# Two attention + gMLP layers on one core: VectorE's share of the exponentials as two addends instead of five, planner latencies split, and another spread of units

## The chip, the cores and the metric

The kernel runs on one core of one Trainium2 chip. Five engines run from queues of their own and wait for each other on semaphores: TensorE (PE), VectorE (DVE), ScalarE (ACT), GpSimd (POOL) and SyncE (SP, which issues the DMAs). The metric is the device time of one execution in microseconds, lower is better; times given are medians of several executions.

## The reference, cut to what matters

An attention and a gMLP are applied in turn, twice (two layers, the same weights), to x of 2048 tokens and 512 channels. The attention has 32 query heads of 16 channels that share one key head and one value head:

```python
q = (x @ wq).reshape(B, S, 32, 16).transpose(0, 2, 1, 3)
k = x @ wk                       # one key head for all query heads
v = x @ wv
scores = einsum('bhqd,bkd->bhqk', q, k) * 16 ** -0.5
p = softmax(scores, axis=-1)
o = einsum('bhqk,bkd->bhqd', p, v)
A(x) = o.transpose(0, 2, 1, 3).reshape(B, S, 512) @ wo
# B: z = gelu(x @ w_in); z1, z2 = halves; z2 = layernorm(z2)
#    g = w_sp @ z2 + b_sp;  B(x) = (z1 * g) @ w_out
x = x + A(layernorm(x)); x = x + B(layernorm(x))     # twice
```

For each layer the softmax needs 32 x 2048 x 2048 exponentials, 134 million. They are the largest piece of elementwise work by far.

## The kernel before, in words

**Groups, units, blocks.** The queries of one layer are cut into 32 groups; a group is 2048 columns of (head, query), held as four row groups of 512 columns. The 2048 keys are 16 tiles of 128. A *unit* is one group against one key tile: four score matmuls, each of which gives one *block* of 128 keys x 512 columns in one PSUM bank. Two layers have 2 x 32 x 16 = 1024 units and 4096 blocks. The first four groups of a layer (`attn_first`) run while keys and values are still being made, in stretches of key tiles that `KEYS` lists; the other 28 (`attn_rest`) run one after another over all 16 key tiles.

**Who takes the exponential.** Most units go through `push_unit`: ACT reads two or three banks at once (two slots, of three and of two banks) and writes exp of them as bf16 into `P_ring` (line 824), and PE then multiplies the block by the values `V_aug` into the accumulator bank `PVB` (line 841). The tables `ON_DVE`, `UNITS` and `FIRST_DVE` name the units that go through `push_unit_dve` instead, 160 of them, 80 in each layer: one in each of the first four groups, three in each of the next twenty, two in each of the last eight.

**How DVE makes an exponential.** For each of the four blocks one `tensor_scalar` (line 872) adds a constant to the scores in PSUM and writes the result as int16 into a tile of `big`. Scores are already scaled so that 128 units are one power of two; the int16 pattern read as bf16 is then 2 to the power of the score, with the fraction taken linearly. To mend that, four more tiles are made from the first by adding 26, 51, 77 and 102 to the int16 patterns (line 881, 128x2048 each), and PE sums all five tiles with values that carry the weights `PH_W` (`V_ph`, line 887): five passes of four matmuls for each unit. The ring of tiles in `big` has six tiles (five in the last eight groups).

**What sets the order.** Nothing is ordered by hand. `_Graph.schedule` simulates the engines with a duration `dur` and a latency `lat` for each operation, takes at each moment the ready operation with the lowest priority number, and so writes one fixed instruction list for each engine; semaphores keep it right whatever the true durations. When PE would idle too long it puts in fillers (`add_zeros`, line 639, which add zero to the accumulator, and the matmuls of ones at line 631). `dve` gives VectorE's operations a duration and no latency; the exponential has `0.065 + n * 0.4267`; a PSUM bank comes free when the latencies of all its operations are over.

**Beside the attention** DVE also normalises (lines 709 to 725), evacuates the output of a group (line 935; line 932 in the first groups), and serves the gMLP: projections (1051, 1077), statistics (1124, 1126, 1131), spatial mixing (1176), and the late mixing (1216, 1221, partly on POOL) after the last group. ACT takes the gelus in place (1087, 1107, 1115).

Of the kernel before, what the change touches and what calls it, by code (L numbers as in the profile page):

```python
# [10 lines left out]
ALU = mybir.AluOpType  # L11
# [25 lines left out]
TILED = 0.217  # L37
SWITCH = 0.105
PE_LAT = 0.20
SEM_LAT = 0.06  # L40
BESIDE = 0.03

HOLDS = 2.5

# [31 lines left out]
class _Op:  # L76
    __slots__ = ("eng", "fn", "dur", "lat", "prio", "seq", "deps", "succ", "nleft", "chan", "chan_val",
                 "inc", "pos", "val", "clock", "t0", "task", "mode", "rows", "work", "opens", "nstart", "due", "chain")

    def __init__(self, eng, fn, dur, lat, prio, seq, chan, task, mode):  # L80
        self.task = task
        self.mode = mode
        self.rows = frozenset()
        self.work = dur
        self.opens = None
        self.eng = eng
        self.fn = fn
        self.dur = dur
        self.lat = lat
        self.prio = prio  # L90
# [12 lines left out]
        self.nstart = 0  # L103
        self.due = 0.0


class _Graph:
# [66 lines left out]
    def schedule(self):  # L174
# [154 lines left out]
        while True:  # L329
            moved = True  # L330
            while moved:
                moved = False
                for e in ENGS:
                    if free[e]:
# [25 lines left out]
                        push(now + us + o.lat + SEM_LAT, 1, o)  # L360
                        at = now + us + o.lat + SEM_LAT
# [11 lines left out]
            while ev and ev[0][0] <= now + 1e-9:  # L373
                _, _, what, x = heapq.heappop(ev)
                if what == 0:
                    free[x] = True
                elif what == 1:
                    for s, k in x.succ:
                        if k == 1:
                            met(s, x)  # L380
                    t = x.task
                    if t is not None:
                        t.left -= 1
                        if t.left == 0:
                            for b in t.banks:
                                bank_free[b] = True
# [75 lines left out]
def bass_interleave_layers__grouped_kv_mqa__mixer_gmlp__prompt_kernel(  # L462
# [127 lines left out]
    def dve(fn, us, r, w, prio=5):  # L590
        return op("dve", fn, us, r=r, w=w, prio=prio)
# [211 lines left out]
    def push_slot(n):  # L803
# [22 lines left out]
        main["last"] = op("act", act_e, 0.065 + n * 0.4267, r=[tk], w=[("P", s0 + k) for k in range(n)], prio=3)  # L826
# [32 lines left out]
    def push_unit_dve(u):  # L859
# [3 lines left out]
        tiles = [phr["base"] + (phr["n"] + a) % phr["ring"] for a in range(NPH)]  # L863
        phr["n"] += NPH
        first_op = None
        for j in range(4):
# [7 lines left out]
                0.66, [tk], BIG(tiles[0]) if j == 0 else [("phj", tiles[0], j)], P_R)  # L874
# [5 lines left out]
        for a in range(1, NPH):  # L880
            dve(lambda e, a=a: e.tensor_scalar(ph16[:, tiles[a], :], ph16[:, tiles[0], :], float(PH_A[a]), None,  # L881
                                               op0=ALU.add), 0.63, base, BIG(tiles[a]), 4)
        for a in range(NPH):
            def pe_pv(e, a=a):
                ins = None
                for j in range(4):
                    ins = e.matmul(bank32(PVB)[32 * j:32 * j + 32, :], V_ph[:, a, kt, :],  # L887
                                   big[:, tiles[a], j * QC:(j + 1) * QC], tile_position=(0, 32 * j), start=False,
                                   stop=False)
                return ins  # L890
            pv_op(pe_pv, (base if a == 0 else BIG(tiles[a])) + [("V", kt)], False, False, TILED)
# [390 lines left out]
    UNITS = {0: (), 1: (4,), 2: (3, 8), 3: (2, 6, 10), 4: (2, 5, 8, 11)}  # L1282
# [6 lines left out]
    FIRST_DVE = ({12: (2,)}, {12: (2,)})  # L1289
# [13 lines left out]
    ON_DVE = [0] * NFIRST + [3] * 20 + [2] * 8  # L1303
# [64 lines left out]
```

## Time and profile before

| | |
|---|---|
| time, median of 3 (range) | 1753.39 us (1752.82 to 1754.59) |
| span of the profiled execution, first to last instruction | 1750.5 us |
| median less that span | 2.9 us |
| PE / DVE / ACT / POOL busy | 95% / 77% / 94% / 5% |
| granted TensorE clock, mean | 0.997 |
| exponentials on ACT, instructions and busy | 1383, 1571.3 us |
| exponentials on DVE, instructions and busy | 1280, 838 us |
| blocks on ACT / on DVE | 3456 / 640 |

The profile shows one execution. Its span is 1750.5 us; the time of an execution holds some microseconds around the span, and the median is 2.9 us above it. A busy share is a mean over stages: there are two stretches without exponentials, at the change of layers and at the end. Instructions of ACT and DVE overlap their successors a little, so a mean duration is longer than the distance between two starts. "PE busy" counts fillers and modelled ends.

### The profile page before, as it was taken

What the parts mean: (1) busy time and instruction counts of PE and PEld (TensorE: products, weight loads), DVE (VectorE), ACT (ScalarE), POOL (GpSimd) and SP (SyncE); (2) the same over time, 40 slices, a digit from 0 to 9 for tenths busy, and PEclk for the clock granted to TensorE, in tenths of its full rate; (3) what the DMA queues carried; (4) which work ended last, traced back from release to release, by engine and by line L of the source; (5) the groups of instructions that cost most, each with busy time, mean ns of one, the idle gap of its engine ahead of it and who ended that gap; (6) DMA issues with size and microseconds to landing.
All of it is one profiled execution on the core that took longest, in us unless ns stands there. A gap on an engine that the chain in (4) does not pass through costs nothing.

```text
span 1750.5 us, 44624 instructions
## 1 busy us (share of the span) xinstructions
PE 1664.3 (95%) x20010; PEld 579.3 (33%) x20010; DVE 1356.0 (77%) x2457; ACT 1637.6 (94%) x1425; POOL 90.4 (5%) x142
## 2 busy tenths in 40 slices
PE   8899999999999999999999999999999999999989
PEld 4332233332333333333432222333333333333334
DVE  8668788888877778675775987888888887766767
ACT  7999999999999999999659999999999999999970
POOL 2000000000000000000430000000000000000012
PEclk9999999999999999999999999999999999999999
DMA  6841000000100302335410000000000112033263
GB/s 185 225 103 49 1 1 2 1 2 25 41 14 20 106 23 70 124 96 161 144 53 19 2 2 1 2 1 2 7 26 7 53 46 88 15 110 110 98 224 120
DMA packets 94816, 104.22 MB, mean 60 GB/s; under 512 B 39072, under 2 KB 64288, under 8 KB 94624
## 3 DMA queue, kind: packets, MB, share of 16 engines
q1 hardware_dynamic: 94624, 101.37, 18.5%
q8 instruction: 156, 2.56, 0.6%
q14 instruction: 36, 0.29, 0.1%
HBM read 61.51 MB, written 39.85 MB: 58 GB/s over the span
## 4 chain that ended last, share of the span: by engine, by line
ACT 75%; PE 22%; DVE 1%; DMA 1%; issue 0%; SPq 0%; POOL 0%; DVEq 0%
ACT P_ring L824 73%; PE ps_all L613 6%; PE ps_all L800 6%; PE ps_all L618 4%; PE ps_all L841 3%; PE ps_all L887 2%; ACT z2n L1087 1%; PE ps_all L639 1%; ACT z1c L1115 0%; PE ps_all L721 0%; DVE big L1216 0%; DVE xn L714 0%; DMA X<-in_A_x_dram 0%; DVE big L1176 0%; DMA big<-gp_scratch 0%
## 5 line engine op out<-in xcount | busy, mean ns | idle before, releaser
L824 ACT ACTIVATE P_ring<-ps_all 128x1536 bf16<-128x1536 f32 (+1 forms) x1383 | 1571.3, 1325 | 56.5 <-PE ps_all L800 55.2
L800 PE MATMUL ps_all<-qT,kT_rep 32*128 32x512 bf16 x4096 | 637.5, 385 | 69.1 <-ACT P_ring L824 55.8
L872 DVE TENSOR_SCALAR big<-ps_all 128x512 int16<-128x512 f32 x640 | 421.8, 686 | 84.5 <-PE ps_all L800 80.2
L881 DVE TENSOR_SCALAR big<-big 128x2048 int16<-128x2048 int16 x640 | 416.2, 682 | 25.0 <-PE ps_all L887 23.8
L800 PEld LDWEIGHTS ps_all<-qT,kT_rep 32*128 32x128 bf16 x4096 | 159.1, 91 | 586.4 <-ACT P_ring L824 451.7
L841 PE MATMUL ps_all<-P_ring,V_aug 128*32 128x512 bf16 x3456 | 333.4, 389 | 0.8 <-DVE big L926 0.5
L887 PE MATMUL ps_all<-big,V_ph 128*32 128x512 bf16 x3200 | 265.0, 385 | 0.6 <-DVE big L872 0.4
L841 PEld LDWEIGHTS ps_all<-P_ring,V_aug 128*32 128x32 bf16 x3456 | 84.6, 93 | 180.7 <-issue 167.2
L639 PE MATMUL ps_all<-ones,zeros 128*32 128x512 bf16 x1320 | 115.0, 388 | 0.0
L887 PEld LDWEIGHTS ps_all<-big,V_ph 128*32 128x32 bf16 x3200 | 75.8, 95 | 90.5 <-issue 36.1
L613 PE MATMUL ps_all<-xnTA,z2n 128*32 128x512 bf16 x1344 | 92.5, 381 | 0.0
L697 POOL TENSOR_SCALAR ve<-mv 128x1 f32<-128x1 f32 (+3 forms) x40 | 10.6, 266 | 1577.3 <-DVE mv L710 1349.9
L962 DVE TENSOR_TENSOR X<-ps_all,X 128x512 bf16<-128x512 f32 x64 | 44.1, 688 | 40.0 <-PE ps_all L618 26.8
L935 DVE CAST oT<-ps_all 128x512 bf16<-128x512 f32 x56 | 38.7, 690 | 38.2 <-PE ps_all L841 38.0
L1176 DVE TENSOR_TENSOR big<-ps_all,big 128x512 f32<-128x512 f32 x56 | 38.3, 689 | 36.8 <-PE ps_all L613 36.5
L1176 DVE TENSOR_TENSOR big<-ps_all,bsp 128x512 f32<-128x512 f32 x56 | 38.5, 688 | 25.1 <-PE ps_all L613 24.6
L613 PE MATMUL ps_all<-w_in_r,xo 128*32 128x448 bf16 x960 | 57.3, 354 | 0.1
L618 PE MATMUL ps_all<-w_out_r,z1c 128*128 128x512 bf16 x224 | 54.2, 380 | 2.8 <-DVE z1c L1221 2.8
L1051 DVE CAST z2n<-ps_all 128x448 bf16<-128x448 f32 x60 | 37.4, 624 | 24.4 <-PE ps_all L613 22.6
L613 PE MATMUL ps_all<-xo,w_in_r 128*32 128x256 bf16 (+1 forms) x1120 | 52.4, 316 | 0.0
L618 PE MATMUL ps_all<-big,z2n 128*128 128x512 bf16 (+1 forms) x224 | 49.4, 366 | 1.3 <-DVE z2n L1131 1.3
L1077 DVE CAST z1c<-ps_all 128x512 bf16<-128x512 f32 (+2 forms) x56 | 36.6, 657 | 16.4 <-PE ps_all L613 13.6
(97 smaller groups left out, 1130.8 us busy)
## 6 DMA issues: line engine op xcount, KB each, us to landing
gp_scratch<-big SPq DMA_DIRECT2D x112, 256.0 KB, 2.0
big<-gp_scratch SPq DMA_DIRECT2D x105, 256.0 KB, 3.0
z1c<-in_B_w_sp_dram SPq DMA_DIRECT2D x16, 512.0 KB, 5.6
wspt_scratch<-z1c SPq DMA_DIRECT2D x16, 512.0 KB, 5.4
xnTA<-wspt_scratch SPq DMA_DIRECT2D x16, 384.0 KB, 4.1
big<-wspt_scratch SPq DMA_DIRECT2D x8, 512.0 KB, 5.8
z2n<-wspt_scratch SPq DMA_DIRECT2D x4, 768.0 KB, 4.8
z1c<-wspt_scratch SPq DMA_DIRECT2D x4, 768.0 KB, 5.6
```

The source lines that it names most:

```text
L613: ins = e.matmul(out_[32 * j:32 * j + 32, :], lhs[:, 32 * j:32 * j + 32], rhs, tile_position=(0, 32 * j), start=start, stop=stop)
L618: return e.matmul(out_, lhs, rhs, start=start, stop=stop)
L639: ins = e.matmul(bank32(PVB)[32 * j:32 * j + 32, :], zeros[:, 0:32], mv, tile_position=(0, 32 * j), start=False, stop=False)
L800: return e.matmul(out, kT_rep[32 * j:32 * j + 32, a, u[1] * P:(u[1] + 1) * P], qT[32 * j:32 * j + 32, q, :], tile_position=(32 * j, 0), st ...
L824: return e.activation(P_ring[:, s0:s0 + n, :], bank32(b0, n).rearrange("p (k q) -> p k q", k=n), ACTF.Exp, scale=E_SCALE)
L841: ins = e.matmul(bank32(PVB)[32 * j:32 * j + 32, :], V_aug[:, kt, :], P_ring[:, s, :], tile_position=(0, 32 * j), start=first, stop=last)
L872: o = dve(lambda e, j=j, tk=tk: e.tensor_scalar(ph16[:, tiles[0], j * QC:(j + 1) * QC], bank32(tk.bank), PH_BIAS, 0.0, op0=ALU.add, op1=AL ...
L881: dve(lambda e, a=a: e.tensor_scalar(ph16[:, tiles[a], :], ph16[:, tiles[0], :], float(PH_A[a]), None, op0=ALU.add), 0.63, base, BIG(tiles ...
L887: ins = e.matmul(bank32(PVB)[32 * j:32 * j + 32, :], V_ph[:, a, kt, :], big[:, tiles[a], j * QC:(j + 1) * QC], tile_position=(0, 32 * j), ...
L935: dve(lambda e: e.tensor_copy(oT[:, par, :], bank32(PVB)), 0.69, ["pvb"], [("oT", par)], 0)
L962: dve(lambda e: e.tensor_tensor(X[:, t, :], bank32(tk.bank), X[:, t, :], ALU.add), 0.69, [tk, ("X", t)], [("X", t)], prio)
L1176: dve(lambda e, part=part, tk=tk: e.tensor_tensor(part, bank32(tk.bank), part if st else bsp[:], ALU.add), 0.69, [tk] + ([] if st else ["b ...
```

## The change

The exponential on DVE gets another form. The bits are made as before, but with the bias 127 x 128 and without a correction. Two addends replace the five shifted tiles: the *whole power* (bits AND 0x7F80, that is 2^e), and the *bits times their own mantissa*: the mantissa as a number from 1 to 2 (bits AND 0x7F, OR 0x3F80), multiplied in bf16 with the bits read as bf16, which is 2^e (1+f)^2. PE sums the two with weights 0.671875 and 0.330078125, so a unit takes two passes of values instead of five, and two bitwise `tensor_scalar` and one `tensor_tensor` on 128x2048 instead of four additions. A unit holds three tiles of the ring instead of five.

181 units instead of 160 go to DVE, by a table for each layer and group. In layer 0 groups 4 to 23 have 71 units (60 before), groups 24 to 31 have 13 (16), and the first four groups two each (one). In layer 1 they have 65 (60), 20 (16), and one each as before.

The planner's figures change too: DVE's operations count 0.085 less as duration and get that as latency, the exponential becomes `0.051 + n * 0.4267` with a latency of 0.185, and a bank that ACT reads comes free without that latency.

```diff
-NPH = 5
-PH_A = (0, 26, 51, 77, 102)
-PH_W = (0.828125, 0.71875, 0.625, 0.54296875, 0.47460938)
+NPH = 2
+PH_W = (0.671875, 0.330078125)
-PH_BIAS = 127.0 * 128.0 - 128.0 * 2.102375911
+PH_BIAS = 127.0 * 128.0
+DVE_LAT = 0.085
+ACT_LAT = 0.185
+UNITS = {0: (), 1: (4,), 2: (3, 8), 3: (2, 6, 10), 4: (2, 5, 8, 11), 5: (2, 4, 7, 9, 12)}
+FIRST_DVE = ({4: (2,), 12: (2,)}, {12: (2,)})
+ON_DVE = ((0, 0, 0, 0, 3, 4, 3, 3, 4, 5, 3, 4, 4, 4, 4, 3, 4, 3, 4, 3, 3, 3, 3, 4, 2, 1, 3, 2, 1, 2, 1, 1),
+          (0, 0, 0, 0, 4, 4, 4, 4, 4, 3, 3, 2, 3, 3, 4, 4, 2, 3, 3, 2, 4, 2, 3, 4, 3, 2, 3, 1, 3, 3, 2, 3))
...
+                        if o.task is not None:
+                            push(now + us + (o.lat if o.free_lat is None else o.free_lat) + SEM_LAT, 3, o.task)
...
     def dve(fn, us, r, w, prio=5):
-        return op("dve", fn, us, r=r, w=w, prio=prio)
+        return op("dve", fn, max(us - DVE_LAT, 0.06), r=r, w=w, prio=prio, lat=DVE_LAT)
...
-        main["last"] = op("act", act_e, 0.065 + n * 0.4267, r=[tk], w=[("P", s0 + k) for k in range(n)], prio=3)
+        main["last"] = op("act", act_e, 0.051 + n * 0.4267, r=[tk], w=[("P", s0 + k) for k in range(n)], prio=3,
+                          lat=ACT_LAT)
+        main["last"].free_lat = 0.0
...
-        for a in range(1, NPH):
-            dve(lambda e, a=a: e.tensor_scalar(ph16[:, tiles[a], :], ph16[:, tiles[0], :], float(PH_A[a]), None,
-                                               op0=ALU.add), 0.63, base, BIG(tiles[a]), 4)
-        for a in range(NPH):
+        bits = ph16[:, tiles[0], :]
+        dve(lambda e: e.tensor_scalar(ph16[:, tiles[1], :], bits, 0x7F80, None, op0=ALU.bitwise_and), 0.69, base,
+            BIG(tiles[1]), 4)
+        dve(lambda e: e.tensor_scalar(ph16[:, tiles[2], :], bits, 0x7F, 0x3F80, op0=ALU.bitwise_and,
+                                      op1=ALU.bitwise_or), 0.69, base, BIG(tiles[2]), 4)
+        dve(lambda e: e.tensor_tensor(big[:, tiles[2], :], big[:, tiles[0], :], big[:, tiles[2], :], ALU.mult), 1.22,
+            base + BIG(tiles[2]), BIG(tiles[2]), 4)
+        for a in range(2):
             def pe_pv(e, a=a):
...
-                                   big[:, tiles[a], j * QC:(j + 1) * QC], tile_position=(0, 32 * j), start=False,
+                                   big[:, tiles[1 + a], j * QC:(j + 1) * QC], tile_position=(0, 32 * j), start=False,
...
-            on_dve = UNITS[ON_DVE[gi]]
-            phr["ring"] = NRING if gi < SHORT_RING else NPH
+            on_dve = UNITS[ON_DVE[now["layer"]][gi]]
+            phr["ring"] = NRING if gi < SHORT_RING else 5
...
-    UNITS = {0: (), 1: (4,), 2: (3, 8), 3: (2, 6, 10), 4: (2, 5, 8, 11)}
-    FIRST_DVE = ({12: (2,)}, {12: (2,)})
-    ON_DVE = [0] * NFIRST + [3] * 20 + [2] * 8
```

More of the change, by code (lines that the diff above doesn't have):

```diff
@@ L89, in __init__ @@
         self.lat = lat
+        self.free_lat = None
         self.prio = prio
@@ L380, in schedule @@
                             met(s, x)
[L381 to L386, printed above, removed]
+                elif what == 3:
+                    x.left -= 1
+                    if x.left == 0:
+                        for b in x.banks:
+                            bank_free[b] = True
         assert done == len(self.ops), (done, len(self.ops))
@@ L862, in push_unit_dve @@
         assert not first and not last
-        tiles = [phr["base"] + (phr["n"] + a) % phr["ring"] for a in range(NPH)]
-        phr["n"] += NPH
+        tiles = [phr["base"] + (phr["n"] + a) % phr["ring"] for a in range(3)]
+        phr["n"] += 3
         first_op = None
```

6 lines of the change are left out of this document (3 added, 3 removed).

## The prediction, written before the changed kernel ran

> **What bounds the kernel now.** I read the page's busy shares and chain first, then the costliest groups, the waits, and last the stretches of time by themselves.
>
> ```profile
> span 1750.5 us, 44624 instructions
> ...
> PE 1664.3 (95%) x20010; PEld 579.3 (33%) x20010; DVE 1356.0 (77%) x2457; ACT 1637.6 (94%) x1425; POOL 90.4 (5%) x142
> ...
> ACT 75%; PE 22%; DVE 1%; DMA 1%; issue 0%; SPq 0%; POOL 0%; DVEq 0%
> ...
> L824 ACT ACTIVATE P_ring<-ps_all 128x1536 bf16<-128x1536 f32 (+1 forms) x1383 | 1571.3, 1325 | 56.5 <-PE ps_all L800 55.2
> ...
> L872 DVE TENSOR_SCALAR big<-ps_all 128x512 int16<-128x512 f32 x640 | 421.8, 686 | 84.5 <-PE ps_all L800 80.2
> L881 DVE TENSOR_SCALAR big<-big 128x2048 int16<-128x2048 int16 x640 | 416.2, 682 | 25.0 <-PE ps_all L887 23.8
> ...
> L887 PE MATMUL ps_all<-big,V_ph 128*32 128x512 bf16 x3200 | 265.0, 385 | 0.6 <-DVE big L872 0.4
> ...
> L639 PE MATMUL ps_all<-ones,zeros 128*32 128x512 bf16 x1320 | 115.0, 388 | 0.0
> ```
>
> PE has the largest busy share, but the chain that ended last is 75% ACT, and ACT's exponentials sit idle for only 56.5 us in all. PE's 95% holds 115.0 us of fillers, which the planner writes only where PE would rest. The waits say which of the two waits for the other:
>
> ```profile
> PEld ps_all L800 <- ACT P_ring L824: 451.7, 1110, 2.0
> ...
> ACT P_ring L824 <- PE ps_all L800: 55.2, 31, 16.7
> ```
>
> The score matmuls wait 1110 times for ACT to free a slot; ACT waits 31 times for scores. Stretch by stretch, busy us and instructions (first PE, weight loads, DVE, ACT, POOL, the granted clock and the DMAs; then ACT's exponentials alone; then DVE's lines 872 and 881 alone):
>
> ```profile
> 125.00:605.00 480.00, 457.74 (x5647) 147.45 (x5646) 398.39 (x715) 478.26 (x420) 6.43 (x10) 1.00 0.06 20
> 220.00:393.00 173.00, 164.21 (x2073) 53.92 (x2069) 146.25 (x270) 172.89 (x151) 5.30 (x8) 1.00 0.01 2
> 985.00:1464.00 479.00, 458.51 (x5703) 149.19 (x5695) 397.25 (x712) 476.23 (x417) 5.72 (x10) 1.00 0.05 16
> ```
> ```profile
> 393.00:605.00 212.00, 211.94 (x189) 1.00 0.10 34
> ```
> ```profile
> 125.00:605.00 480.00, 160.13 (x243) 1.00 0.06 20
> 220.00:393.00 173.00, 52.36 (x80) 1.00 0.01 2
> 985.00:1464.00 479.00, 156.09 (x237) 1.00 0.05 16
> ```
> ```profile
> 125.00:605.00 480.00, 159.00 (x244) 1.00 0.06 20
> 220.00:393.00 173.00, 53.23 (x82) 1.00 0.01 2
> 985.00:1464.00 479.00, 159.03 (x244) 1.00 0.05 16
> ```
>
> 125 to 605 us is groups 4 to 23 of layer 0, 985 to 1464 the same of layer 1. ACT is busy for 99.6% of the one and 99.4% of the other. So a block taken from ACT is time saved, as long as DVE, at 83% in both, carries what it gets.
>
> **The price of a block on ACT.** From 393 to 605 us ACT does nothing but exponentials: 189 instructions, slots of three and two banks in turn, so 472.5 blocks in 211.94 us, 0.449 us each. The kernel's mean, 1571.3 us over 3456 blocks, is 0.455, with the small waits in it. I take 0.449. The change moves 181 - 160 = 21 units, 84 blocks: 37.7 us (38.2 by the mean). By place: four units more in layer 0's first groups (7.2 us), 11 more in its groups 4 to 23 (19.8), 3 fewer in 24 to 31 (minus 5.4); in layer 1, 5 more (9.0) and 4 more (7.2).
>
> **The price of a unit on DVE.** Back to back, operations start closer than they last:
>
> ```profile
> 1064.23 3.09 DVE L881 TENSOR_SCALAR big<-big 128x2048 int16<-128x2048 int16 x5
> ```
>
> (3.09 - 0.68) / 4 = 0.603 us for line 881; a block (line 872) lasts 4 ns longer, and I use 0.61 for both. A unit before is eight such, 4.9 us. After, the four block operations stay. The two bitwise ones have the shapes and types of line 881, and one of them has two operations in one instruction. The nearest rows for that, and for the product of two 16-bit tensors, are
>
> ```profile
> L1216 DVE TENSOR_TENSOR big<-ps_all,big 128x512 f32<-128x512 f32 x49 | 32.0, 681 | 5.0 <-PE ps_all L618 4.2 <-DMA big<-gp_scratch 0.8
> ...
> L1131 DVE TENSOR_SCALAR z2n<-z2n,mv,rs 128x896 bf16<-128x896 bf16 x32 | 14.7, 502 | 2.7 <-POOL rs L699 2.4
> ...
> L1216 DVE TENSOR_TENSOR big<-ps_all,big 128x256 f32<-128x256 f32 x7 | 2.6, 417 | 0.0
> ...
> L684 DVE TENSOR_TENSOR fold<-ident 128x64 bf16<-128x64 bf16 x1 | 0.2, 203 | 0.0
> ...
> L685 DVE TENSOR_TENSOR fold<-fold 128x32 bf16<-128x32 bf16 x1 | 0.2, 174 | 0.1
> ```
>
> Line 1216 costs (681 - 417) / 256 = 1.03 ns per element and 153 ns fixed; at that rate 2048 elements are 2.27 us. Line 881 streams 2048 in 682 - 153 = 529 ns, four times as fast. Line 1131 does two operations on 896 16-bit elements in 502 ns, where the slow rate would give 1.08 us, so two operations in one instruction don't lose the fast rate. Bitwise: between 0.68 and 2.27 us; I take 0.68, that of the row with the same operands. Product: between 0.68 (as one source) and 2.27 (line 1216's rate); I take 153 + 2 x 529 = 1.21, because two 16-bit sources must be read where line 881 reads one; less 0.07 of overlap, 1.14. A unit after: 6 x 0.61 + 1.14 = 4.8 us.
>
> Against my 1.21 speak lines 684 and 685, the only rows of such a product: 203 - 174 = 29 ns for 32 elements, 0.9 ns each, which would make 2.0 us and a unit 5.6. They are single records of short operations. The Trainium skill ("VectorE: DVE Perf Modes", section "The perf-mode tier table") holds that `tensor_tensor` on bf16 in SBUF goes at half of `tensor_scalar`'s top rate and gives 1224 ns for 2048 elements; no run here shows that yet. By the page the sum below stays as it is; by the two short rows it would be some 20 us higher, as worked out with the rivals.
>
> **DVE's load.** In 125 to 605 us DVE's other work is 398.39 - 160.13 - 159.00 = 79.3 us. With 71 units it needs 79.3 + 71 x 4.8 = 420 us; ACT needs 480 - 19.8 = 460. DVE is then 91% loaded, 96% if it keeps today's looser mean of (160.13 + 159.00) / 480 operations = 0.665 us. In layer 1: 397.25 - 156.09 - 159.03 = 82.1, plus 65 x 4.8, is 394 of 470 us, 84%. The tightest stretch is 220 to 393 us, groups 8 to 14: other work 40.7, units from 21 to 27, so 170 us of DVE work where ACT needs 173 - 6 x 1.8 = 162. That is 8 us too much. What can slide out of it is the normalising and projecting (lines 1051 to 1131) of tiles that are not mixed until later; the next groups have slack. I charge half, 4 us, as new waits of ACT; the ends are 0 and 20 (8 here, and some 12 in like stretches of four-unit groups that I can't tell apart from the trace).
>
> **PE.** Passes of values fall from 3200 to 1448 matmuls: 1752 at 265.0 / 3200 = 0.083 us, 145 us less; `P_ring`'s fall by 84. The instruction order has 1832 of line 639's fillers instead of 1320, 45 us. PE waits for ACT already, so I cost this at nothing: between minus 15 us (a bit less than half of the 55.2 - 16.7 = 38.5 us of ACT's waits for scores without the longest) and zero. What grows if DVE is late is PE standing at a pass of values, with the next scores behind it in PE's queue and ACT waiting for those; that is inside the 4 us above.
>
> **The last stage** changes only by its order:
>
> ```profile
> 1697.82 2.32 PE L631 MATMUL ps_all<-ones 128*128 128x512 bf16 x10
> 1699.97 0.59 PE L618 MATMUL ps_all<-w_out_r,z1c 128*128 128x512 bf16 x2
> 1703.37 5.79 PE L618 MATMUL ps_all<-w_out_r,z1c 128*128 128x512 bf16 x26 [2.80 <-DVE z1c L1221]
> ```
>
> Here PE burns 10 fillers and waits 2.80 us. In the new order eight real matmuls of the next part stand in place of most of those fillers: 8 x 0.22 = 1.8 us gained; between 0 and 4. The planner's split latencies change no instruction, only which comes first; elsewhere I cost that at nothing, between minus 5 and plus 5 us, because PE's and DVE's order is hidden as long as ACT has a full slot. No DMA is added or taken out on SP or POOL. A smaller `V_ph` (two weights) and fewer memsets are under 1 us, beside the first loads.
>
> **Sum.** 1750.5 - 37.7 + 4 - 1.8 = 1715.0 span; plus the 2.9 us that lie around it, 1718 us against the median of 1753.39, 2% faster.
>
> **The rivals.**
> *DVE can't keep up in the crowded groups.* All 20 us of DVE's excess become waits of ACT: 1718 + 16 = 1734. For it: 105% load from 220 to 393 us, and the passes of values are behind the evacuation of a group. Against it: the ring now holds two units, and neighbours with two or three units give the time back.
> *PE's relief shortens ACT's small waits.* Up to 15 us, so 1703. For it: ACT's mean of 0.455 against 0.449. Against it: fillers fill most of the room.
> *Slower: the new value operations don't run at the fast rate,* in groups 4 to 23 of layer 0. If the two bitwise take 153 + 2 x 529 ns, a unit is 4.8 + 1.06 = 5.9 us, DVE needs 79.3 + 71 x 5.9 = 498 us for the stretch instead of 460: 38 us more, and layer 1's 82.1 + 65 x 5.9 = 466 just fits its 470. That gives 1752, no change: at 5.9 us a unit the gain is gone. The product at line 1216's rate alone (1.06 more) makes the same; by lines 684 and 685 (0.8 more) it is 1718 + 22 = 1740. From there on it is slower: bitwise and product both so make 7.0 us, 116 us in layer 0 and 67 in layer 1, about 1900; the bitwise at the slow rate (1.59 more each) 8.0, 187 and 132 us, about 2035. For it: no row shows a bitwise operation. Against it: same operands as line 881.
> *The change doesn't do what it says:* the blocks leave ACT for certain, by count; what could fail is only their worth, which is the second and fourth case.
>
> **How the numbers follow.** Forecast (1708 to 1727) 0.61; DVE late (1727 to 1748) 0.16; small waits shorter (1697 to 1708) 0.10; slow rates, 0.13, of which 0.02 end within 0.2% (3.5 us, about what a measurement tells from no change) and 0.11 above. Faster 0.87, same 0.02, slower 0.11. The range from 1702 to 1748 leaves out the slow rates and the lowest part of the third case.
>
> **What would show it.** ACT: 1349 exponentials, about 1534 us busy, and idle before them still near 55 us (60 with the 4). Bitwise at 0.68 us and product near 1.21; 1.2 and 2.3 would mean the slow case. From 220 us on, more `ACT P_ring <- PE` waits if DVE is late, with PE standing at passes of values. DVE busy near 1440 us. The stage after the last exponential some 2 us shorter. I am wrong if the operations are slow, or if ACT's waits grow by more than 20 us.

## The result, and the profile after

The changed kernel takes 1727.58 us (median of 4, 1726.11 to 1728.45) against 1753.99 for the kernel before (the three executions of the table above and a fourth): a ratio of 0.9843, with a 95% interval from 0.9824 to 0.9863. The forecast was 1718 in a range from 1702 to 1748. So the direction and the range held, and 9.6 us are to be found. The profiled execution took 1728.45 us, its span 1726.7, which is 23.8 less than before. (One execution of one experiment, the planner's choice of closed fillers below, took 7195 us with each matmul some four times as long as in the others; it is left out of that experiment's time.)

The page of the changed kernel: busy time, the granted clock in 40 slices, the chain by engine, and the groups that answer to those shown before the prediction.

```profile
span 1726.7 us, 41922 instructions
...
PE 1623.9 (94%) x18678; PEld 558.7 (32%) x18678; DVE 1425.2 (83%) x2444; ACT 1602.1 (93%) x1391; POOL 93.7 (5%) x136
...
PEclk8899999999999999999998998999999999999999
...
ACT 74%; PE 20%; DVE 4%; issue 1%; POOL 0%; DMA 0%; SPq 0%; DVEq 0%
...
L832 ACT ACTIVATE P_ring<-ps_all 128x1024 bf16<-128x1024 f32 (+1 forms) x1349 | 1535.5, 1340 | 71.9 <-PE ps_all L808 70.5
...
L882 DVE TENSOR_SCALAR big<-ps_all 128x512 int16<-128x512 f32 x724 | 473.4, 683 | 50.1 <-PE ps_all L808 46.9
...
L895 DVE TENSOR_TENSOR big<-big 128x2048 bf16<-128x2048 bf16 x181 | 219.0, 1210 | 0.7
L647 PE MATMUL ps_all<-ones,zeros 128*32 128x512 bf16 x1832 | 161.7, 397 | 0.0
...
L901 PE MATMUL ps_all<-big,V_ph 128*32 128x512 bf16 x1448 | 131.0, 396 | 1.7 <-DVE big L895 1.0
L891 DVE TENSOR_SCALAR big<-big 128x2048 int16<-128x2048 int16 x181 | 123.3, 681 | 9.2 <-PE ps_all L901 8.2
L893 DVE TENSOR_SCALAR big<-big 128x2048 int16<-128x2048 int16 x181 | 122.6, 677 | 0.3
```

Line 832 is the old line 824, ACT's exponentials: 35.8 us less busy, and 15.4 us more idle before them (71.9 against 56.5), nearly all behind scores. Lines 891, 893 and 895 are the three new operations, 901 the passes of values (3200 matmuls before), 647 the fillers (1320 before). The stretches between the same evacuations (groups 4 to 23 of layer 0, groups 8 to 14 of it, groups 4 to 23 of layer 1) have these busy times, with the granted clock third from the end:

```profile
127.00:588.00 461.00, 429.27 (x4983) 139.96 (x4982) 435.92 (x731) 457.72 (x401) 9.46 (x10) 0.99 0.08 21
221.00:377.00 156.00, 143.04 (x1632) 44.67 (x1629) 150.11 (x245) 154.60 (x138) 3.16 (x2) 0.99 0.04 12
976.00:1450.00 474.00, 446.53 (x5306) 142.73 (x5303) 411.82 (x690) 468.26 (x410) 8.40 (x10) 0.98 0.06 19
```

In the tight stretch ACT is still busy for 154.60 of 156 us, so DVE, though itself busy for 96%, does not hold it up. What is new stands in the first 128 us. Two windows of the kernel before, then the same two after:

```profile
0.00:64.00 64.00, 55.13 (x646) 25.88 (x650) 51.72 (x116) 51.66 (x46) 11.75 (x36) 1.00 0.74 207
64.00:128.00 64.00, 58.28 (x655) 21.88 (x647) 40.05 (x70) 62.92 (x57) 0.00 (x0) 0.97 0.58 145
```
```profile
0.00:64.00 64.00, 56.01 (x551) 21.68 (x551) 53.37 (x114) 45.01 (x39) 8.84 (x28) 0.81 0.35 102
64.00:128.00 64.00, 58.84 (x641) 22.30 (x640) 54.00 (x90) 62.12 (x56) 1.26 (x2) 0.95 0.66 176
```

In the first window the granted clock falls from 1.00 to 0.81, ACT does 6.7 us less work, and PE is as busy as before. In the second DVE has 14 us more work than before; whether that matters is taken up with e12 below. In windows of 4 us:

```profile
32.00:36.00 4.00, 3.55 (x42) 1.37 (x40) 3.83 (x11) 4.00 (x4) 1.28 (x2) 1.00 0.62 135
36.00:40.00 4.00, 3.78 (x50) 2.20 (x46) 3.57 (x8) 4.00 (x5) 0.00 (x0) 1.00 0.76 213
```
```profile
28.00:32.00 4.00, 3.36 (x36) 1.18 (x36) 4.00 (x9) 4.00 (x4) 0.00 (x0) 0.99 0.14 31
32.00:36.00 4.00, 3.53 (x24) 0.78 (x24) 3.29 (x8) 3.76 (x5) 0.00 (x0) 0.50 0.02 4
36.00:40.00 4.00, 4.00 (x24) 0.61 (x23) 2.76 (x6) 2.81 (x3) 0.00 (x0) 0.50 0.00 0
40.00:44.00 4.00, 4.00 (x32) 2.16 (x29) 3.07 (x5) 2.61 (x3) 0.00 (x0) 0.50 0.00 0
```

The first pair is before, the rest after. From 32 us on the matmuls run at half rate: PE does 24 of them where it did 42 and 50, is "busy" for 3.53 and 4.00 of 4 us, and ACT, with 2.81 and 2.61 of 4 us, waits for scores. The clock's records give 11 such spells before the last exponential, 78.5 us in all; the kernel before has 10.2 us. Which comes first can be read from the trace: in the 3.4 us ahead of each of the 11 spells ACT is still busy for 99 to 100%, while PE is busy for only 44 to 82%, and ahead of ten of them what PE waits for longest is ACT, which has to free a slot (ahead of the one at 936 us it is DVE). So ACT does not lack scores before the clock falls; it lacks them after.

**Where the 23.8 us come from.** ACT's exponentials start 1.3305 us apart (three banks) or 0.9045 us (two) when nothing holds them; what is beyond that, from start to start, I count as wait. A wait is put down to a half-rate spell if the exponential ahead of it starts in the spell or in the microsecond behind it.

| | before | after | difference |
|---|---|---|---|
| exponentials at their own pitch | 1544.9 | 1507.3 | -37.6 |
| ACT's waits in half-rate spells | 4.4 | 27.5 | +23.1 |
| ACT's waits elsewhere | 35.4 | 31.2 | -4.2 |
| the one long wait at the change of layers | 16.8 | 16.3 | -0.5 |
| after the last group | 72.0 | 68.0 | -4.0 |
| all else (start, gelus) | 77.0 | 76.4 | -0.6 |
| span | 1750.5 | 1726.7 | -23.8 |

So the blocks gave what they were priced at, and against that stand 23 us more of waits that begin where PE's clock falls. The last stage, PE's rows of the changed kernel:

```profile
1717.01 0.82 PE L639 MATMUL ps_all<-ones 128*128 128x512 bf16 x3 [1.44 <-DVE big L1230]
1717.67 4.70 PE L626 MATMUL ps_all<-w_out_r,z1c 128*128 128x512 bf16 x21
```

Three fillers and a wait of 1.44 us stand where ten and 2.80 us stood.

### The profile page after: what moved, and what is told of

The parts are those of the page before. It is cut to its first block, busy times and chain, and to the rows that moved or that the text cites. A ratio compares the mean times of both kernels' runs of the same rounds, so it can differ in the third digit from the quotient of the medians.

```text
span 1726.7 us, 41922 instructions
## 1 busy us (share of the span) xinstructions
PE 1623.9 (94%) x18678; PEld 558.7 (32%) x18678; DVE 1425.2 (83%) x2444; ACT 1602.1 (93%) x1391; POOL 93.7 (5%) x136
## 4 chain that ended last, share of the span: by engine, by line
ACT 74%; PE 20%; DVE 4%; issue 1%; POOL 0%; DMA 0%; SPq 0%; DVEq 0%
ACT P_ring L832 73%; PE ps_all L621 6%; PE ps_all L808 5%; PE ps_all L626 4%; PE ps_all L851 3%; PE ps_all L901 1%; ACT z2n L1101 1%; PE ps_all L647 1%; DVE big L1230 1%; DVE st L1138 0%; DVE big L882 0%; DVE xn L722 0%; DVE z2n L1145 0%; DVE st L717 0%; PE ps_all L746 0%
## 5 line engine op out<-in xcount | busy, mean ns | idle before, releaser
L832 ACT ACTIVATE P_ring<-ps_all 128x1024 bf16<-128x1024 f32 (+1 forms) x1349 | 1535.5, 1340 | 71.9 <-PE ps_all L808 70.5
L808 PE MATMUL ps_all<-qT,kT_rep 32*128 32x512 bf16 x4096 | 653.3, 391 | 79.5 <-ACT P_ring L832 61.9
L882 DVE TENSOR_SCALAR big<-ps_all 128x512 int16<-128x512 f32 x724 | 473.4, 683 | 50.1 <-PE ps_all L808 46.9
L851 PE MATMUL ps_all<-P_ring,V_aug 128*32 128x512 bf16 x3372 | 325.6, 395 | 1.4 <-DVE oT L949 0.8
L895 DVE TENSOR_TENSOR big<-big 128x2048 bf16<-128x2048 bf16 x181 | 219.0, 1210 | 0.7
L647 PE MATMUL ps_all<-ones,zeros 128*32 128x512 bf16 x1832 | 161.7, 397 | 0.0
L901 PE MATMUL ps_all<-big,V_ph 128*32 128x512 bf16 x1448 | 131.0, 396 | 1.7 <-DVE big L895 1.0
L891 DVE TENSOR_SCALAR big<-big 128x2048 int16<-128x2048 int16 x181 | 123.3, 681 | 9.2 <-PE ps_all L901 8.2
L893 DVE TENSOR_SCALAR big<-big 128x2048 int16<-128x2048 int16 x181 | 122.6, 677 | 0.3
L647 PEld LDWEIGHTS ps_all<-ones,zeros 128*32 128x32 bf16 x1832 | 41.2, 95 | 74.0 <-issue 67.7
L621 PE MATMUL ps_all<-w_in_r,xo 128*32 128x448 bf16 x960 | 56.5, 355 | 0.5 <-DVE z1c L1091 0.3
L901 PEld LDWEIGHTS ps_all<-big,V_ph 128*32 128x32 bf16 x1448 | 36.1, 96 | 47.7 <-issue 24.1
```

The lines of the kernel that those rows point to most:

```text
L621: ins = e.matmul(out_[32 * j:32 * j + 32, :], lhs[:, 32 * j:32 * j + 32], rhs, tile_position=(0, 32 * j), start=start, stop=stop)
L647: ins = e.matmul(bank32(PVB)[32 * j:32 * j + 32, :], zeros[:, 0:32], mv, tile_position=(0, 32 * j), start=False, stop=False)
L808: return e.matmul(out, kT_rep[32 * j:32 * j + 32, a, u[1] * P:(u[1] + 1) * P], qT[32 * j:32 * j + 32, q, :], tile_position=(32 * j, 0), st ...
L832: return e.activation(P_ring[:, s0:s0 + n, :], bank32(b0, n).rearrange("p (k q) -> p k q", k=n), ACTF.Exp, scale=E_SCALE)
L851: ins = e.matmul(bank32(PVB)[32 * j:32 * j + 32, :], V_aug[:, kt, :], P_ring[:, s, :], tile_position=(0, 32 * j), start=first, stop=last)
L882: o = dve(lambda e, j=j, tk=tk: e.tensor_scalar(ph16[:, tiles[0], j * QC:(j + 1) * QC], bank32(tk.bank), PH_BIAS, 0.0, op0=ALU.add, op1=AL ...
```

## The experiments

My theory was that PE's clock took the missing part. The rivals were that DVE is late after all, that the planner's figures (which instruction comes first) make the waits, and that a block is worth less than its price. This table has all runs whose profile can be read, counted as above; "layer" is the long wait at the change of layers, "end" the time after the last group; all columns but the time are us of the profiled execution. (In e3 no such wait stands between two exponentials; in e9 there are two, added up.) The time lay in a range that was named beforehand in e2 and e4 alone; the other runs missed all their ranges, e5, e8, e11 and e12 by less than 2 us.

| kernel | time, us (ratio to before) | at half rate | waits in it | waits elsewhere | layer | end |
|---|---|---|---|---|---|---|
| before | 1753.4 | 10.2 | 4.4 | 35.4 | 16.8 | 72.0 |
| changed kernel | 1727.6 (0.984) | 78.5 | 27.5 | 31.2 | 16.3 | 68.0 |
| e8 before, new planner figures | 1765.8 (1.008) | 34.1 | 11.5 | 47.2 | 17.4 | 67.6 |
| e4 changed, 160 units | 1751.6 (0.999) | 13.7 | 3.8 | 35.8 | 18.4 | 67.7 |
| e3 changed, old planner figures | 1790.1 (1.021) | 47.8 | 25.7 | 90.3 | 0 | 72.4 |
| e7 unit of 6.0 us | 1834.5 (1.047) | 71.7 | 44.0 | 114.5 | 16.1 | 69.9 |
| e2 one unit in the first groups | 1730.3 (0.986) | 30.7 | 10.5 | 34.3 | 17.4 | 70.2 |
| e1 fillers up to 0.65 | 1741.0 (0.993) | 34.1 | 12.4 | 39.1 | 21.3 | 80.8 |
| e5 23 groups of fillers in the first stage | 1725.7 (0.985) | 58.0 | 20.5 | 33.5 | 17.4 | 68.0 |
| e6 526 groups of fillers | 1770.7 (1.010) | 44.4 | 17.9 | 80.8 | 16.3 | 68.0 |
| e9 three empty passes a unit | 1800.4 (1.027) | 47.8 | 15.8 | 35.4 | 46.4 | 111.4 |
| e10 190 fillers at closed accumulators | 1753.2 (1.000) | 44.4 | 25.1 | 57.3 | 17.2 | 68.0 |
| e12 closed fillers planned, true work | 1727.0 (0.985) | 27.3 | 7.6 | 39.2 | 21.5 | 69.8 |

### The parts of the change

**The planner's figures alone (e8),** in the kernel before:

```diff
-        return op("dve", fn, us, r=r, w=w, prio=prio)
+        return op("dve", fn, max(us - 0.085, 0.06), r=r, w=w, prio=prio, lat=0.085)
...
-        main["last"] = op("act", act_e, 0.065 + n * 0.4267, r=[tk], w=[("P", s0 + k) for k in range(n)], prio=3)
+        main["last"] = op("act", act_e, 0.051 + n * 0.4267, r=[tk], w=[("P", s0 + k) for k in range(n)], prio=3,
+                          lat=0.185)
+        main["last"].free_lat = 0.0
```

> The kernel before (five shifted tiles, 160 units) with the new planner figures alone. If the figures bring something by themselves: the last stage's 2 to 4 us, 1749 to 1752 us. If they cost clock (fillers on the accumulator fall from 1320 to 1173): 1753 to 1765 us.

Measured 1765.84 us, ratio 1.0075 (1.0053 to 1.0098): 12.8 us slower than before (1753.06 there). Half-rate time is 24 us more and ACT's waits are 19 us more, while the last stage is 4.4 us shorter: the gain that I saw there belongs to the figures.

**Two addends with the old 160 units (e4).**

```diff
-FIRST_DVE = ({4: (2,), 12: (2,)}, {12: (2,)})
-ON_DVE = ((0, 0, 0, 0, 3, 4, 3, 3, 4, 5, ...
+FIRST_DVE = ({12: (2,)}, {12: (2,)})
+ON_DVE = ([0] * 4 + [3] * 20 + [2] * 8,) * 2
```

> Two addends and the new planner figures, but the 160 units of before in their old places. If a block on ACT is the whole price, this has none of the 37.7 us: 1754 less the last stage's 2 to 4 us, 1748 to 1753 us. If the addends themselves help by relieving TensorE and VectorE (ACT's small waits shorter), 1735 to 1745 us; if the relief of TensorE costs clock, 1754 to 1765 us.

Measured 1751.61 us, ratio 0.9992 (0.9981 to 1.0003). Groups 4 to 23 of the two layers:

```profile
125.00:605.00 480.00, 451.90 (x5366) 144.21 (x5365) 395.67 (x662) 478.12 (x419) 7.51 (x10) 1.00 0.05 18
985.00:1464.00 479.00, 453.09 (x5402) 145.45 (x5394) 393.49 (x659) 478.28 (x420) 5.61 (x10) 1.00 0.05 18
```

The clock stays at 1.00 and ACT is busy 99.6% and 99.8%. So two passes in place of five don't by themselves bring the half rate; with these planner figures it comes when 21 more units go to DVE. The order counts as well: e8 has five passes, 160 units and 34.1 us at half rate. By this way the change falls into three steps: figures +12.8, addends -14.2 (1765.8 to 1751.6; ACT's waits fall by 19 us), units -24.0 (1751.6 to 1727.6). The last is the step of the 84 blocks: -37.6 by their pitch, +23.7 of waits at half rate, and some -7 of smaller terms in the profiled spans. A block is worth its price; other waits take part of it back.

**The new form and units with the old planner figures (e3):** the diff of e8 the other way round.

> The changed kernel (two addends, 181 units) with the planner figures of before: no latency split for VectorE, 0.065 + n * 0.4267 for the exponential. Its list has 2619 fillers on the accumulator instead of 1832. Theory 'planner': the split figures make the planner believe that TensorE is busier than it is, it writes fewer fillers, and the clock falls; with the old figures the clock is near 1.0 and the time 1716 to 1722 us. Theory 'VectorE' and any theory that blames the units or addends: 1727 us or more, since the order made with old figures is no better: 1727 to 1735 us.

Measured 1790.08 us, ratio 1.0207 (1.019 to 1.0224), 62 us more than the changed kernel, with the same instructions beside fillers. That is far above both ranges that were named (to 1735 us). ACT waits 90.3 us outside the half-rate spells; 33.8 us of all its waits lie in groups 8 to 14 of layer 0. So the figures cost 13 us in the one kernel and save 62 in the other: which order is good depends on the units, and the edit can't be priced by itself.

### How near DVE is to being late

**The first bitwise operation three times (e7),** 1.2 us more for each unit:

```diff
+        for _ in range(2):
+            dve(lambda e: e.tensor_scalar(ph16[:, tiles[1], :], bits, 0x7F80, None, op0=ALU.bitwise_and), 0.69, base,
+                BIG(tiles[1]), 4)
```

> The changed kernel with the first bitwise operation written three times (the output is the same), so that a unit costs VectorE 1.2 us more, 6.0 instead of 4.8; the planner knows of it. It measures what the slow case of the prediction would have cost: groups 4 to 23 of layer 0 need 79.3 + 71 x 6.0 = 505 us of VectorE where ACT needs 460, 45 more; layer 1 472 of 470. The theory that VectorE's load bounds those groups: 1727 + 45 = 1772 us, within 15. If VectorE had room that I don't see: 1727 to 1740 us.

Measured 1834.53 us, ratio 1.0466 (1.0422 to 1.0511). The page's group of exponentials, then the window of groups 8 to 14 of layer 0:

```profile
L832 ACT ACTIVATE P_ring<-ps_all 128x1024 bf16<-128x1024 f32 (+1 forms) x1349 | 1539.1, 1333 | 169.9 <-PE ps_all L808 168.5
...
L894 DVE TENSOR_SCALAR big<-big 128x2048 int16<-128x2048 int16 x362 | 247.8, 685 | 0.0
```
```profile
225.00:442.00 217.00, 187.75 (x2378) 62.48 (x2375) 210.45 (x362) 167.13 (x143) 8.06 (x8) 0.96 0.04 14
```

Here DVE is late: 210.45 of 217 us busy, ACT 167.13. The stretch is 61 us longer than in the changed kernel (216.3 against 155.2) for 28 x 1.2 = 34 us of work on DVE. So the slow rival was real, and its price less than half of what it is: my 5.9 us for a unit gave 34 us above the forecast, this unit of 6.0 stands 107 us above the changed kernel. The waits lie elsewhere than in the changed kernel: 53 of the 158.5 us are in these seven groups, where the changed kernel has 3.5 us. The two causes are not cleanly apart, though: 24 of the 53 us begin in half-rate spells, which this kernel has there too.

### The half rate

**One unit instead of two in layer 0's first groups (e2),** 177 units:

```diff
-FIRST_DVE = ({4: (2,), 12: (2,)}, {12: (2,)})
+FIRST_DVE = ({12: (2,)}, {12: (2,)})
```

> The changed kernel without the four additional units in layer 0's first groups (177 units; 16 blocks back on ACT, 7.2 us by the price of a block). Theory 'VectorE': these units crowd the first stage; without them ACT's waits there fall from 11 to about 2 us and the time is 1725 to 1727 us, as the 7.2 us come back. Theory 'clock': what counts is the matmul work around 30 us and 85 us, not the units; if it still is too small without them the granted clock still falls to 0.5 there, the waits stay above 6 us and the time is 1730 to 1735 us.

Measured 1730.34 us, ratio 0.9864 (0.9849 to 0.9879). The first 64 us:

```profile
0.00:64.00 64.00, 56.68 (x627) 25.51 (x630) 56.20 (x125) 49.64 (x44) 10.12 (x30) 0.95 0.51 147
```

The clock there rises from 0.81 to 0.95. Sixteen blocks come back to ACT, 7.2 us by their price, and the waits at half rate fall by 17 us. In the first 126.6 us half-rate time falls from 30.7 to 6.8 us and all of ACT's waits from 11.0 to 5.1, which is between the two theories (2 us, and above 6); the span is 0.9 us shorter, the median 2.8 us longer than the changed kernel's. So the four units in the first groups, priced at -7.2, are worth between nothing and 3 us.

**More fillers by the planner's own rule (e1).** The planner wants work on PE for 0.55 of any 3.4 us, by its figures; here 0.65:

```diff
-WARM = 0.55
+WARM = 0.65
```

> The changed kernel with the planner's filler share WARM at 0.65 instead of 0.55 (2812 fillers on the accumulator instead of 1832, nothing else). Theory 'clock': the 9 us lost in layer 0's first stage are TensorE at half its granted clock, because too little matmul work stands in its list there; then the clock from 0 to 128 us stays near 1.0 instead of 0.85, ACT's waits there fall from 11 to under 4 us, and the time is 1717 to 1721 us. Theory 'VectorE': the first stage is late because DVE is full (105 of 128 us busy); fillers change nothing or cost, 1727 to 1732 us, and ACT's waits stay at 11 us.

Measured 1741.03 us, ratio 0.9929 (0.9914 to 0.9944). The half-rate time falls to 34.1 us, but 27.3 of it lie in the first stage, where the fillers did not end it: ACT's waits there stay at 10.5 us, and the run can't tell the two theories apart. The last group ends where it did (1658.2 us against 1658.6). The added time is in the last stage (80.8 us against 68.0), where mixing products that lost their place to fillers now stand, with PE waiting:

```profile
1692.60 0.61 PE L639 MATMUL ps_all<-ones 128*128 128x512 bf16 x1 [4.06 <-DVE big L1230]
```

**Fillers that the planner doesn't know of (e5, e6).** They are put into the finished list behind a pass of values: in e5 between 22 and 100 us, whatever the work; in e6 from 22 us on, where the work of the last 3.4 us is under 75%. The diff is that of e5, without the test of the work. The traces show 23 groups of four more than in the changed kernel for e5, not the 34 that were named, and 526 for e6.

```diff
+            if not (o.prio == 1 and o.mode == 2 and o.opens is None and 22.0 <= o.t0 < 100.0):
+                continue
...
+            z = _Op("pe", lambda e: self.zeros(e, 2), WARM_OP, PE_LAT, FILLER, o.seq, None, None, 2)
...
+            pe.append(z)
```

> The changed kernel with every engine's order as it is, and in TensorE's list one more filler (four matmuls of zeros into the open accumulator) behind each pass of values between 22 and 100 us of layer 0, 34 in all; the planner doesn't see them. Theory 'clock': the half-rate spells of 32 to 50, 56 to 62 and 84 to 90 us go, ACT's waits in layer 0's first four groups fall from 11.0 to under 4 us, and the time falls by 6 to 9 us, to 1719 to 1722. Theory 'VectorE or order': the waits come from the order, more matmuls only lengthen TensorE's queue: 1727 to 1735 us.

> As the run before, but over the whole attention of both layers, behind a pass of values wherever the list holds less than 75% of matmul work in the last 3.4 us by the planner's times (some 540 fillers of four). Theory 'clock': the spells near 172, 290, 940, 970, 1045, 1065, 1212 and 1508 us go too, with some 16 us of waits of ACT; mean granted clock above 0.99; 1705 to 1715 us. If TensorE's list has no room for them, ACT waits for scores behind fillers and the time is 1728 to 1760 us.

Measured 1725.71 us (0.9847, 0.9829 to 0.9866) and 1770.67 (1.0102, 1.0061 to 1.0142). The fillers of e5 stand at 51 us and later, so none is in the largest spell (32 to 49 us) that they were meant for. They did not end the half rate: 30.7 us of the first stage are at half rate in both kernels, so e5 tests neither theory. Up to 51 us the two lists are the same, and yet the spells there lie at 17 to 21 and 34 to 45 us in e5: they are not tied to a place in the list alone. Those of e6 brought the half-rate time to 44.4 us, and cost 50 us elsewhere: ACT waits 80.8 us outside the spells. Each filler stands in PE's queue ahead of scores; that this is why ACT waits is argued, not shown.

**Three passes with zero weights for each unit (e9),** so that PE has five again, known to the planner:

```diff
+        for a in range(3):
...
+                    ins = e.matmul(bank32(PVB)[32 * j:32 * j + 32, :], zeros[:, 0:32],
+                                   big[:, tiles[2], j * QC:(j + 1) * QC], tile_position=(0, 32 * j), start=False,
+                                   stop=False)
```

> The changed kernel with three further passes per unit that multiply the unit's tile by weights of zero: TensorE gets back the five passes of before, VectorE and ACT keep the change (two addends, 181 units, new planner figures; the planner knows of the passes). Theory 'clock by emptied list': the half-rate spells come because two passes leave too little matmul work around the change of groups, where the accumulator is closed and no filler can stand; with five passes only a few spells are left (mean granted clock above 0.99), ACT's waits fall from 75 to 55 to 62 us, and the time is 1712 to 1720 us. Theory 'VectorE's order': the passes only make TensorE's list longer, 1728 to 1745 us.

Measured 1800.38 us, ratio 1.0273 (1.0248 to 1.0298). Half-rate time 47.8 us and its waits 12 us less; layer 0 ends 4.5 us earlier. But gMLP matmuls are pushed to the end of each layer (852 of them start after the last group's evacuation, 349 in the changed kernel): 30 us more waiting at the change and 43 us more after the last group. PE's room is not free for the taking.

**Fillers where the accumulator is closed (e10, e11, e12).** Between a group's last pass of values and the next group's first the planner has no place for a filler that adds to the accumulator. In e10 190 that overwrite it, after it was evacuated, are put into the finished list; in e11 the planner itself has that choice (18 used); in e12 the V products, which have 16 columns and weights of the full array, count in its account of work with 0.007 us each instead of 0.06; that is the time of 16 columns at 0.42 ns, not a part of the array, as the expectation below has it.

```diff
+            if not bs and evac in fin:
+                o = _Op("pe", lambda e: self.over(e), WARM_OP, PE_LAT, FILLER, len(self.ops), None, None, 2)
+                o.deps[evac] = 1
...
+        for o in t2.ops:
+            if o.eng == "pe":
+                o.work = o.dur * 0.007 / 0.06
```

The diff is of e11 and e12; the last three lines are in e12 alone.

> The changed kernel with every order as it is, and 190 fillers of four matmuls that write the accumulator bank between its evacuation and the next group's first pass (which overwrites them), two behind each score operation that stands there in TensorE's list; the planner doesn't see them. Theory 'clock by emptied list': the spells after the first stage (172, 290, 940, 970, 1045, 1065, 1212, 1508 us) mostly go, some 16 us of ACT's waits with them, and the fillers themselves cost up to 0.08 us each as in the run with sparse fillers, 15 us: 1715 to 1728 us, mean granted clock above 0.987. If the spells don't depend on this work: clock 0.977 and 1735 to 1745 us.

> The changed kernel, with one more choice for the planner: where PE would rest between a group's last pass of values and the first pass of the next group, it may write fillers into the closed accumulator once that has been evacuated (72 matmuls there, 1956 ordinary ones; 1832 in the changed kernel). Theory half rate: the spells that begin in those rests go; time at half rate before the last exponential falls from 78 us to 30-45, ACT's waits in it from 27 us to 10-16, and with the 68 us last stage unchanged the time is 1712-1722 us. Rival, the order: the waits come from which instruction the planner puts first, and the new list is only another draw: waits outside half rate 35-60 us, time 1728-1750 us. In this list some gMLP matmuls stand after the last exponential that stood before it, so either theory allows a last stage up to 8 us longer.

> As the run before, and the products for V, 16 columns each, are counted in the planner's account of PE's work by the share of the array that they fill (0.007 us each instead of 0.06), so that it adds fillers in the first stage, near 28-60 us, where the changed kernel has 30.7 us at half rate (92 matmuls in the closed accumulator, 1876 ordinary). Theory half rate: half-rate time in the first 110 us falls below 15 us and ACT's waits there from 11 us to 4-6, so 3-6 us less than the run before, 1708-1720 us. Rival, the order: first-stage spells change, time doesn't follow: 1728-1750 us.

Measured: e10 1753.24 us (1.0003, 0.9986 to 1.0019): as with e6 the half-rate time falls, and ACT waits 26 us more elsewhere. e11 1723.8, the median of three executions from 1722.67 to 1724.83 (0.983, 0.9805 to 0.9856), with a mean granted clock of 0.989 to 0.992 against 0.977; its profile is of the execution that was left out, so its waits can't be told apart. e12 1726.99 (1722.25 to 1730.22; 0.9849, 0.9816 to 0.9882). Of e12 the clock in slices, two windows, and the wait of ACT:

```profile
PEclk9999999999989999999999999999999999999999
```
```profile
0.00:64.00 64.00, 54.94 (x626) 22.57 (x626) 58.63 (x127) 50.83 (x45) 10.21 (x30) 0.97 0.39 115
64.00:128.00 64.00, 59.00 (x661) 21.82 (x657) 54.12 (x91) 63.87 (x58) 0.00 (x0) 1.00 0.53 147
```
```profile
L853 ACT ACTIVATE P_ring<-ps_all 128x1536 bf16<-128x1536 f32 (+1 forms) x1349 | 1534.5, 1334 | 68.3 <-PE ps_all L829 66.5
```

What the first theory says of the place is shown: with the clock at 0.97 and 1.00, ACT does 7.6 us more work in the first 128 us, its waits there fall from 11.0 to 2.5 us, and the fourth group ends at 118.1 us instead of 126.6. DVE has more to do there than in the changed kernel (58.63 and 54.12 us busy against 53.37 and 54.00), so its load alone does not make the waits of the first stage. What that theory says of the whole is not: the waits at half rate fall by 19.9 us, yet the span only by 3.2, since ACT waits 8.0 us more elsewhere and 5.2 more at the change of layers, and the last stage is 1.8 us longer. Both expectations for the time miss e12 by a little (1708 to 1720 the one, 1728 to 1750 the other), and e11 likewise. Neither kernel can be told from the changed one by its time: the intervals overlap.

## Why the prediction was right or wrong

**The bound and the price of a block: right.** 84 blocks are 37.6 us by the pitch of the exponentials (37.7 predicted), 35.8 us of busy time. ACT leads the chain as before.

**The price of a unit: right to the last digit that the profile shows.** Bitwise 0.681 and 0.677 us (0.68 taken), product 1.210 (1.21), blocks 0.683. The two short rows that spoke against the product (0.9 ns per element) were misleading. The sentence from the Trainium skill ("VectorE: DVE Perf Modes", section "The perf-mode tier table"), 1224 ns, agrees with 1210 within 1.2%. DVE is busy for 1425.2 us where I expected 1440.

**DVE late in crowded groups, +4: wrong, it is nothing.** I had 170 us of DVE's work in a stretch where ACT needs 162. I had also miscounted: the table gives groups 8 to 14 of layer 0 28 units and not 27, so it should have been 175 us against 160, an excess of 15 and not 8. In the profile DVE is busy for 150.11 us of its 156, of which 134.7 are the units' (lines 882, 891, 893 and 895 in that window). So 15 us of other work stayed there, where 40.7 had been: it slid out by more than the excess. ACT's waits there are 3.5 us, against 2.3 before, and 1.6 of them stand in a half-rate spell. But the cover is thin, as e7 shows, and the rival of slow rates had its break-even and its prices too kind: the sum over twenty groups let DVE use slack that the crowded seven don't have. Nor do the 22 us for the two short rows follow from it: 79.3 + 71 x 5.6 = 477 us against 460 are 17.

**PE's relief at nothing, from -15 to 0: wrong in sign for what decides.** This is the step that failed. I looked at PE as a server with more room, and so gave the relief no end above zero. The runs show two things in its place. With 160 units the two addends are worth -14.2 us, near my lower bound (e8 to e4). With 181 units PE has rests in which its clock falls to half, and the waits that begin there are 23.1 us more than before: by the account more than the whole difference to the forecast (+23.1 here, less 4 for DVE, 4.2 for other waits, 2.2 for the last stage, 1.0 for small terms, and 2 us because the median lies nearer to the profiled span than before: 9.7). It is an account and not a gain to be had: in e12 most of that term went and the time stayed. Nor is it shown that the rests come from the lighter passes and not from the order: e4 has the lighter passes and 13.7 us at half rate, e8 the five passes and 34.1. Why 181 units leave PE such rests, the runs don't settle; where the rests lie is seen: in the first stage, and between a group's last pass and the next one's first.

**The planner's figures at nothing, within 5: wrong.** Alone they cost 12.8 us (e8); without them the change is 62 us slower (e3). I argued that the order on PE and DVE is hidden as long as ACT has a full slot; at PE's 94% it isn't. The two errors, figures +12.8 and addends -14.2, cancel in the sum, which is luck.

**The last stage, -1.8: right in kind, too small,** -4.0; three fillers stay of ten, and the figures alone make it (67.6 us in e8; 72.4 without them in e3).

**The first groups, -7.2: gone.** By e2 they are worth 0 to 3 us.

**The signs named beforehand:** 1349 exponentials with 1535.5 us (about 1534 said). ACT's idle time before them 71.9 us, outside the 55 to 60 that I named, and that was the sign of the missing term. The median lies 0.6 us above the stretch that I gave the forecast (1708 to 1727), in the one for a late DVE, and not for that reason. That it lies so near is in part luck: 23.1 us that I had not foreseen met 13.4 us of small terms the other way.

## What to carry to other kernels

Before PE's relief is costed at nothing, look whether PE keeps its clock: read the granted clock in short windows, and remember that a PE that is 100% busy in the profile may be running at half rate. In a kernel that an order in advance drives at 94% on two engines, fillers, latencies and the spread of work have one price together, and each alone may have the other sign. A rival that DVE is overloaded is to be priced over the most crowded groups, not over the mean of a long stretch.

## What the runs showed of the hardware

**The clock goes by windows of 3.413 us, and by how much of the array works in them.** In all profiles the half-rate spells are whole multiples of 3.413 us (the last of a trace is cut off by its end). I gave each matmul its columns times 0.417 ns from its start on (in the last stage's rows before, 26 matmuls of 512 columns take 5.79 us and 10 take 2.32, so 0.42 ns a column), times the part of the 128 x 128 array that its weights fill, a quarter for scores and for passes of values, and summed by window. Over 13 profiles, for windows at full rate between the first and the last exponentials:

```
work of the window / 3.413 us   next window at half rate   next at full rate
under 0.30                      38                         0
0.30 to 0.34                    15                         1
0.34 to 0.36                    17                         3
0.36 to 0.38                    13                         18
0.38 to 0.40                    2                          54
0.40 to 0.45                    0                          304
over 0.45                       0                          5711
```

Where the windows begin differs from execution to execution, as the spells of e5 show. The point lies near 0.36 to 0.37: one threshold there puts 16 of the 6176 windows on the wrong side. If every matmul counts in full, whatever part of the array it fills, 80 of the 85 windows ahead of a half-rate one hold more than 0.45, and the best threshold has 81 windows on the wrong side. The Trainium skill ("TensorE: Matmul & The Clock Gate", section "What's actually happening") tells of a gate with two rates, half and full, decided over a free-running window of 3413 ns; the traces agree in length and rates. Its advice to avoid idle gaps over about 3 us (section "Why this matters for your kernels") is not enough here: in the 3.4 us ahead of the changed kernel's 11 spells PE's longest rests are 0.2 to 1.9 us. What counts is the sum of small tiles' work, and a score matmul fills a quarter of the array.

**The price:** ACT waits 0.35 us for each microsecond at half rate in the changed kernel (27.5 of 78.5), 0.28 to 0.43 in before, e1, e2, e4, e5, e6, e8, e9 and e12, and 0.54 to 0.61 in e3, e7 and e10. Not all of a wait in a spell need come from the clock, as e7 shows.

**Matmuls four times as long without a record of it.** In the execution of e11 that took 7195 us the score matmuls have these times, against 391 ns in the changed kernel, under a granted clock of 1.00; ACT's and DVE's instructions nearly kept theirs. No run shows the cause.

```profile
L826 PE MATMUL ps_all<-qT,kT_rep 32*128 32x512 bf16 x4096 | 2209.5, 1430 | 1.4 <-DVE big L900 1.4
```
